# Splitting a 2048-point transform 64 by 32 instead of 128 by 16 in a fused long-convolution and feed-forward kernel

## The chip, the cores and the metric

The kernel runs on one core of a Trainium2 chip. A core has TensorE (PE), which multiplies matrices on an array of 128 rows by 128 columns and writes to eight PSUM banks of 512 float32 columns; VectorE (DVE) and ScalarE (ACT), which work element by element and empty the banks; GpSimd (POOL) and SyncE (SP), which issue most of the transfers. The metric is the device time of one execution in microseconds (us).

## The reference

S = 2048 positions, D = 640 channels, F = 1728 hidden units, all in bfloat16. One layer norm feeds two branches. Branch A multiplies a short causal filter of `k` (four taps for each channel) with `v`, convolves the product along the positions with a filter as long as the sequence (by an FFT of twice the length), adds a skip term and multiplies with the normed input. Branch B is a feed-forward network with gelu, followed by silu. The result is the input plus the product of the branches.

```python
def _A_ref(q, k, v, shift_k, ssm_k, ssm_D):
    k_pad = jnp.pad(k, ((0, 0), (ks - 1, 0), (0, 0)))
    for t in range(ks):
        k_shift = k_shift + k_pad[:, t:t + S, :] * shift_k[:, ks - 1 - t][None, None, :]
    kv = k_shift * v
    kv_f = rfft(pad(kv, S)); kf_f = rfft(pad(ssm_k, S))      # along the positions, length 2 S
    y = irfft(kv_f * kf_f)[:S]                               # in bfloat16
    return q * (y + kv * ssm_D)
def _B_ref(x, w1, b1, w2, b2):
    return gelu(x @ w1 + b1) @ w2 + b2
x = A_q
xn = _layernorm(x)
return x + _A_ref(xn, A_k, A_v, ...) * silu(_B_ref(xn, ...))
```

## The kernel before, in words

**Layout.** Position 16 p + j lies on partition p as row j of 640 channels (`x_v`, `k_v`, `v_v`, `out_v`). `area` is a pool of 48 slots of two such rows; every intermediate of branch A takes a slot (`pair`, `flat`) or a run of columns over two slots (`span`), with a count of uses after which the slot comes free (`Slots`).

**The transform.** The long convolution is a transform in two stages, a product, and the inverse in two stages, all by matmuls.

- *First stage* (`f1`, line 582; steps `kf` for the filter, `uf` for the signal): for each of the 16 rows n2 the 128 partitions are multiplied with a 128x128 matrix of cosines (`WA`) and one of sines (`WB`). A step is one bank, a third of 1280 columns (`EDGES`: 428, 426, 426), and has one or two matmuls. There are 48 steps for each operand. Each step's bank is emptied by `f1_out` on ACT (`.a` in the plan) or DVE (`.d`), and the lines go to DRAM (`scrK`, `scrU`) by POOL's queue.
- *Second stage* (`blocks`, line 445; steps `ff` for the filter, `mu` for the signal, `ma` and `mb` for the inverse): the lines come back from DRAM with 128 of them across the partitions. The transform of 16 points, real and imaginary part, is block-diagonal in blocks of 32, so a step is four matmuls of 32x32 by 512 columns; the digit of `TURNS` says by how many blocks a step rotates its outputs, so that steps next to each other can use different blocks of the array. 40 steps of each of the four kinds make 160 groups, 640 matmuls. `product` on DVE multiplies with the filter (40 times plainly, 40 times with real and imaginary part swapped; `swap_load` makes that copy by DMA).
- *Last stage* (`inv2`, lines 745 and 746; steps `y`): after a third trip through DRAM (`scrC`, `cab_load`), a step sums a matmul with `GA` and one with `GB`, both 128x128. `GA` and `GB` are the memory of `WA` and `WB`, filled anew with the inverse's angles: for each of four parts a product, a mask, a sine, an absolute value and a cosine (`i2_*`). `gate` multiplies the bank with the other branch.

**The short filter.** `kv_step` (lines 611 to 628; steps `cv`) works on two rows at a time: four products with the taps, three sums, one product with `v`, 8 pieces x 8 operations of 1280 elements a partition on DVE. The taps are spread over the partitions by matmuls (`tap`), two in the opening (`prologue`) and two later (`late_tap`, steps `em` and `ee`).

**The feed-forward branch** runs in four chunks of 512 positions: `ffn1` (steps `h`, line 498; the 14th of each chunk, line 494, has 64 hidden units and puts two matmuls of 64 columns side by side), gelu on ACT, `ffn2` (steps `g`, line 531, 14 matmuls of 320 columns), silu on ACT, products on POOL and DVE.

**The order.** Nothing is scheduled at run time. After `prologue`, the text `PLAN` lists some 1,100 steps, and each engine and queue does its share of them in that order. SP's queue does the loads (`X`, `K`, `V`, `C`, `B`, `fl`, `ml`, `mk`, `yl`, `q`), POOL's the stores (`ks`, `us`, `ms`, `ys`). A step that needs a bank or a slot waits until it has been emptied. The plan mixes feed-forward steps with steps of branch A.

Of the kernel before, what the change touches and what calls it, by code (L numbers as in the profile page):

```python
# [34 lines left out]
PLAN = """
ir he0 X1 he1 he2 em6 he3 em7 w h13 em5 K1 ls5 ws1 ls4 ls7 em4 K0 h8 ee6.d ee4.a ls6 h10 ee7.a ee5.a he13 cv16 lv1 lr1
cv1 he4 he8 C2 cv0 h6 cv9 he5 lb1 he6 h7 cv2 h12 ln6.d h11 cv8 ln5.d ln4.a h9 he10 ln7.a tt8 he12 B1 cv17 he11 he9 cv3
he7 cv10 cv18 B0 cv11 cv4 cv19 cv20 tt9 s B2 tt6 tt7 te9.a g3 cv21 te6.d cv22 tt5 C1 ge3 C0 ws2 ss te7.d sm g2 g7 cv12
C3 C4 ge2 kt3 V3 kt5 te5.d kt8 V1 d kc5.d kt10 ws0 kt14 K2 ge7 kc3.a te8.d kc10.d kt0 cv5 kf10 kc8.a kc14.a kf24 kt12
ke24.a kt4 kc12.d kf31 V7 kt6 kf11 kf9 ke10.a K3 kc4.d ke31.a kc0.d ke11.a kf44 kf43 V2 ke44.d kt2 kc2.d kc6.a kf17 X3  # L40
ke9.a kf32 ke32.d kf30 kt11 kf42 kt13 kf37 kt7 kc11.d ke30.a ks10 ke17.a kf38 kc13.d V6 ke42.a ke43.a kt9 ke37.d kf16
kf1 kc7.d kt1 gm3.d kf12 ke38.a ke16.a kc9.d kf36 kt15 kf21 ke1.a ke36.a kc1.d kf6 kf29 gm7.d kc15.d kf39 kf25 ke21.a
X2 cv33 V5 kf20 ke6.a kf41 cv32 V0 cv6 cv24 ks12 ke29.a ks14 cv23 cv13 ke25.a cv34 kf15 ke15.a ke41.a cv56 ke20.a ks5
g5 ke12.a kf7 kf13 ge5 cv57 kf14 kf27 kf8 ke39.a ke27.a kf26 kf40 ke8.a cv41 g0 kf28 ke40.a ks13 ke26.a ke14.a cv40
uf13 kf34 ks3 ke7.a kf19 ge0 cv35 ks8 ue13.a kf18 kf35 ke13.a ke18.a ks4 kf45 g4 ke19.a ks6 gm5.d uf17 cv36 ke45.a kf33
ke34.a ke28.a ks9 ke35.a gm0.d kf0 ke33.a cv7 kf23 cv14 V4 cv58 kf47 cv37 ge4 ke23.a ke0.a kf5 kf22 g6 uf4 ks2 ks11
ke5.a cv42 ke47.a ke22.a ks7 ge6 kf4 kf46 uf5 cv15 ls10 ke4.a cv59 uf15 kf3 ke46.a ks15 kf2 cv38 ke3.a ks1 ke2.a cv25
g1 ue4.a uf0 ks0 ue5.a gm6.d fl0 uf3 ue15.a ue17.a ue3.a uf12 cv43 ue12.a uf14 ue14.a uf16 cv39 ue16.a ue0.a cv26 uf1
ue1.a fl9 h21 us1 uf2 ue2.a ls9 us4 ge1 uf11 gm1.d h15 cv44 cv48 cv45 he21 gm2.d cv46 h25 cv27 uf9 cv60 h19 ue11.a uf27
us5 cv47 h16 he15 cv61 he25 uf28 us0 ue9.a he16 cv28 cv62 uf26 h27 ue28.a uf6 fl3 fl8 h20 ue27.a he19 he20 uf25 h17  # L50
he27 uf29 uf10 h23 h26 ue29.a ue6.a uf8 uf7 ue25.a ue26.a ue10.a cv29 ue8.d cv63 fl4 he17 uf34 ue7.a ue34.a he26 h14
uf33 ff1 fl2 ue33.a he14 cv30 cv49 uf32 uf35 uf46 ue46.a fl1 uf42 he23 h22 ue35.a he22 uf44 uf31 ue31.a h18 cv31 uf23
us9 uf24 ue42.a uf30 cv50 ue44.d cv51 uf43 ue32.a ue43.d ue24.a cv52 he18 uf22 fl13 h24 ls11 ue23.a us2 fl15 cv53 fe1.a
uf21 ff11 ue22.a ff7 ue30.a ff8 ls8 us14 he24 g14 uf47 fe11.a ue21.a uf45 fe7.a uf19 ue45.a cv54 g13 ue47.d ge13 cv55
lv2 ue19.d uf18 uf20 ge14 uf38 uf36 us8 us10 ue20.d us3 uf40 gm4.d us11 ue18.a fl14 fl6 uf39 ue39.d us7 ls13 ue38.a
uf41 uf37 ue37.a g9 ue36.a ff6 fl5 ff12 fl12 us15 ue40.d fl7 lr2 lb2 ff20 ln11.d ff2 ff24 ln9.d us6 us12 ue41.a fe8.a
ge9 gm9.d fe20.d fe12.a ff5 ff0 fe24.a fe2.d g11 fe5.a fe0.a ff14 ls14 ln10.d ff13 ff37 ff38 ff33 ff34 ln8.d fe6.a us13
ge11 mk2 ls12 ml2 fe14.a ff16 g15 tt12 fe34.a tt13 fe16.a gm14.p fe38.a tt14 fe37.d tt11 fe33.a ff10 ff35 te12.d te13.d
ff9 ge15 ff3 ff30 fe13.a ml5 te11.d fe9.a te14.d ml3 ff32 g8 tt10 fe3.a ff19 fe35.d ff17 fe30.a ff4 ml4 fe32.a ff31
fe10.a ls15 ff36 gm15.p mu5 lv3 te10.d fe36.a mk5 fe17.a mp5 fe4.a g12 lr3 ff15 mu13 lb3 fe19.d gm13.p mq5 fe31.a  # L60
ln15.d mp13 mu7 mk3 mk4 ge8 ff39 fl11 mu6 ff18 fe39.a gm8.p fe18.a g10 h40 mu14 ml6 mq6 fl10 mq13 ge12 fe15.a ma5 mp6
mp7 ff22 ge10 mq7 mu10 mp14 ff21 mb5 mu9 mq9 he40 h38 fe21.a mk6 mq14 ml1 me5.a mp9 he38 h37 mq10 fe22.a mp10 h29 q2
mu8 he37 ln13.d mu12 mk1 mq8 ma9 he29 ff27 mq12 ml0 mk0 ff23 mp12 mb9 mu15 h35 mq15 mp8 h32 ml8 h34 mu11 fe27.a me9.a
ln12.a mp15 ma8 he35 he32 ml7 ma7 mb7 ma10 fe23.a he34 mu16 mb8 gm10.p ff25 me7.a me8.a ff26 mp11 h39 mu2 mq16 mk8 mu3
mk13 mb10 gm11.p mp16 h33 mk7 mq11 fe26.a ma11 ml10 ma14 fe25.a ff29 mq2 me10.a mb14 mp2 mp3 mk9 mb11 he39 he33 mu20
me14.a mu1 me11.a mq3 mu4 mq4 fe29.a h41 he41 h28 gm12.p mp4 h31 he28 ma15 mp20 ml13 ma4 ff28 mb15 ml12 mu17 mq20 he31
mb4 mp1 mq1 ma3 mb3 mu0 mp0 me4.a h36 fe28.a mp17 me3.a h30 ml9 mu19 ma13 he36 mq0 ma12 me15.a mq17 ma6 mb12 mb13 ma16
mp19 mb6 mu18 mb16 mu34 ml15 mp18 he30 mk12 me13.a g20 ma17 mq19 mq18 me12.a me16.a mu26 ms4 me6.a ms5 mk10 mq34 mu33
# [868 lines left out]
```

## Time and profile before

| | us |
|---|---|
| median of 2 runs | 191.13 (191.09 to 191.18) |
| the profiled execution | 191.78 |
| its span, first to last instruction | 189.8 |
| busy: PE, DVE, ACT, POOL | 183.3, 171.1, 159.1, 59.5 |

The span is what the profile shows of the program; the profiled execution took 2.0 us more than it, and 0.65 us more than the median. A group's row gives line, engine, operation, output and input tiles, shape and count, then the busy time in us, the mean ns of one, and the idle time just before. The matmuls of PE are pipelined: a matmul's duration in a row is longer than the time from its start to the next one's start, and only the latter adds up.

### The profile page before, as it was taken

The numbers are of one execution on the slowest core, as the hardware profiler recorded it, in microseconds if no ns is written. First come the engines' busy times: TensorE is split into PE (matmuls) and PEld (weight loads), VectorE is DVE, ScalarE is ACT, GpSimd is POOL, SyncE is SP. The second block draws the span as 40 slices with busy tenths as digits, with TensorE's granted clock in tenths as the row PEclk, the third lists the DMA queues.
The fourth block names the chain that finished last, engine by engine and source line by source line (L and its number), as shares of the span: only waits on it lengthen the run. The fifth ranks groups of instructions, "written<-read, shape, count | busy, mean of one in ns | idle before, by whom it ended". The sixth has DMA issues, their size and how long they took to land.

```text
span 189.8 us, 4853 instructions
## 1 busy us (share of the span) xinstructions
PE 183.3 (97%) x1811; PEld 110.0 (58%) x1811; DVE 171.1 (90%) x341; ACT 159.1 (84%) x307; POOL 59.5 (31%) x99
## 2 busy tenths in 40 slices
PE   7999999899999999999999999999999999999992
PEld 2486467787765544466665434467563544677671
DVE  6979999999999999899989999999999950689993
ACT  3469999999999999999988999998789599894031
POOL 8539200013546111266043300046159440001050
PEclk9999999999999999999999999999999999999999
DMA  6999999987998999798599899998988859992165
GB/s 186 397 376 311 363 359 405 380 340 231 391 352 329 254 382 378 234 386 337 178 335 318 266 301 337 310 353 287 343 298 284 287 178 290 402 394 114 38 256 195
DMA packets 26399, 57.67 MB, mean 304 GB/s; under 512 B 3016, under 2 KB 14857, under 8 KB 26376
## 3 DMA queue, kind: packets, MB, share of 16 engines
q1 hardware_dynamic: 21872, 39.65, 61.0%
q0 software_dynamic: 4320, 17.70, 25.1%
q8 instruction: 14, 0.23, 0.5%
q14 instruction: 9, 0.07, 0.1%
q10 hardware_dynamic: 184, 0.01, 0.1%
HBM read 33.76 MB, written 18.35 MB: 275 GB/s over the span
## 4 chain that ended last, share of the span: by engine, by line
PE 75%; DMA 16%; ACT 3%; DVE 2%; issue 1%; SPq 1%; DVEq 0%; ACTq 0%
PE banks L531 28%; PE banks L498 21%; DMA w_sb<-in_B_w_dram 11%; PE banks L582 9%; PE banks L445 8%; DMA area<-in_A_ssm_k_dram 5%; PE banks L746 2%; PE banks L745 2%; PE banks L571 2%; ACT area L143 2%; PE banks L482 1%; ACT hT L510 1%; PE banks L494 1%; DVE xn L555 1%; DVE xn L547 0%
## 5 line engine op out<-in xcount | busy, mean ns | idle before, releaser
L143 ACT CAST area<-banks 128x512 bf16<-128x512 f32 (+3 forms) x162 | 78.8, 618 | 5.5 <-PE banks L445 5.5
L531 PE MATMUL banks<-w_sb,hT 128*128 128x320 bf16 (+1 forms) x462 | 66.0, 295 | 0.1
L531 PEld LDWEIGHTS <-hT 128*128 128x128 bf16 x462 | 43.3, 98 | 19.5 <-issue 3.8
L498 PE MATMUL banks<-xnT,w_sb 128*128 128x512 bf16 x230 | 53.5, 379 | 0.0
L704 DVE TENSOR_TENSOR area<-banks,area 128x512 bf16<-128x512 f32 x80 | 48.6, 682 | 0.8 <-PE banks L445 0.4
L498 PEld LDWEIGHTS <-w_sb 128*128 128x128 bf16 x230 | 21.7, 98 | 25.6 <-issue 2.7
L510 ACT ACTIVATE hT<-banks,b_f 128x512 bf16<-128x512 f32 x52 | 33.9, 706 | 1.8 <-PE banks L498 1.0
L539 ACT ACTIVATE sl<-banks 128x320 bf16<-128x320 f32 (+1 forms) x33 | 14.9, 464 | 12.7 <-PE banks L531 10.9
L626 DVE TENSOR_TENSOR area<-area 128x1280 bf16<-128x1280 bf16 x32 | 25.3, 814 | 0.1
L622 DVE TENSOR_TENSOR area<-area 128x1280 bf16<-128x1280 bf16 x24 | 19.3, 816 | 0.0
L730 POOL DMA_DIRECT2D scrC<-area x16 | 11.8, 737 | 23.2 <-DMA area<-area 18.7
L754 DVE TENSOR_TENSOR area<-banks,xn 128x426 bf16<-128x426 f32 (+1 forms) x18 | 10.0, 595 | 9.1 <-PE banks L746 9.1
L597 POOL DMA_DIRECT2D scrK<-area x16 | 8.8, 555 | 28.7 <-DVE area L144 19.1
L445 PE MATMUL banks<-area,mats 32*32 32x512 bf16 x640 | 17.2, 380 | 0.0
L582 PE MATMUL banks<-area,WA 128*128 128x212 bf16 (+1 forms) x64 | 16.5, 299 | 0.0
L547 POOL TENSOR_TENSOR xn<-xn,sl 128x320 bf16<-128x320 bf16 x14 | 11.2, 808 | 15.6 <-ACT sl L539 10.2
L582 PE MATMUL banks<-area,WB 128*128 128x426 bf16 (+1 forms) x64 | 15.8, 299 | 0.0
L608 POOL DMA_DIRECT2D scrU<-area x16 | 8.6, 543 | 20.9 <-ACT area L143 14.5
L445 PEld LDWEIGHTS <-mats 32*32 32x32 bf16 x640 | 6.4, 88 | 10.1 <-issue 8.2
L763 POOL DMA_DIRECT2D out_dram<-area x6 | 3.3, 551 | 26.5 <-DVE area L759 26.5
L144 DVE CAST area<-banks 128x426 bf16<-128x426 f32 (+3 forms) x18 | 10.9, 611 | 0.7 <-ACT area L143 0.5
L452 DVE BATCH_NORM_STATS2 st<-xn 128x6 f32<-128x320 bf16 x24 | 10.4, 477 | 0.0
(108 smaller groups left out, 209.4 us busy)
## 6 DMA issues: line engine op xcount, KB each, us to landing
scrK<-area POOLq DMA_DIRECT2D x16, 320.0 KB, 4.0
scrU<-area POOLq DMA_DIRECT2D x16, 320.0 KB, 5.1
area<-scrK SPq DMA_DIRECT2D x16, 320.0 KB, 6.6
area<-area SPq DMA_DIRECT2D x32, 160.0 KB, 4.4
area<-scrU SPq DMA_DIRECT2D x16, 320.0 KB, 4.4
scrC<-area POOLq DMA_DIRECT2D x16, 320.0 KB, 4.6
area<-scrC SPq DMA_DIRECT2D x16, 320.0 KB, 6.9
area<-in_A_k_dram SPq DMA_DIRECT2D x4, 640.0 KB, 9.4
```

Source lines behind the costliest of these rows:

```text
L143: return nc.scalar.copy(out=out_ap, in_=in_ap)
L445: nc.tensor.matmul(out=out[b, :], lhsT=mats[a, m, a], rhs=rhs[a, :], start=start, stop=stop)
L498: nc.tensor.matmul(out=ps, lhsT=w1_sb[:, t, ft * P:(ft + 1) * P], rhs=xnT[:, t, :], start=(t == 0), stop=(t == DT - 1))
L510: nc.scalar.activation(out=hT[:, ft, :], in_=one(("h", i)), func=ACT.Gelu_apprx_tanh, bias=b1_f[:, ft:ft + 1], scale=1.0)
L531: nc.tensor.matmul(out=ps[:, 0:ws.stop - ws.start], lhsT=hT[0:M, ft, q * P:(q + 1) * P], rhs=w2_sb[0:M, ft, hs.start + ws.start:hs.start + ...
L539: nc.scalar.activation(out=sl[:, ws], in_=one(key)[:, 0:ws.stop - ws.start], func=ACT.Silu)
L547: mul.tensor_tensor(out=xr[:, ws], in0=xr[:, ws], in1=live["sl", i][:, ws], op=ALU.mult)
L582: nc.tensor.matmul(out=ps[:, dst], lhsT=(WA, WB)[r][:, n2, :], rhs=rows[:, n2 % 2, src], start=True, stop=True)
L622: nc.vector.tensor_tensor(out=uc, in0=uc, in1=tmp, op=ALU.add)
L626: nc.vector.tensor_tensor(out=tmp if s else uc, in0=kh[:, r0:r0 + KC, :], in1=w_exp[:, j:j + 1, :].to_broadcast([P, KC, D]), op=ALU.mult)
L704: nc.vector.tensor_tensor(out=p_part(i, x), in0=full(one(("mu", i)), i), in1=span(name, i), op=ALU.mult)
L730: nc.gpsimd.dma_start(out=pair_view(scrC)[g2], in_=pair(("c", g2)))
```

## The change

The 2048 points are split as 64 by 32 instead of 128 by 16. Position 32 p + 16 h + j lies on partition 64 h + p, so each half of the partitions holds the 64 positions of one parity h of the block of 16.

- *First stage*: a matmul multiplies the 64 rows of one half with a 64x128 matrix `W`, whose columns alternate cosine and sine of 64 frequencies. Step i of 48 has half h = i mod 2; the number of matmuls and their columns stay. The angle tables are half as wide.
- *Second stage*: the transform of 32 points with its two parts has blocks of 64 (`QB = 64`), so a group is two matmuls of 64x64 by 512 columns. `TURNS` has other digits, of which the parity counts.
- *Last stage*: a matmul has all 128 rows and 64 columns (`G`), one for each half of the output partitions; nothing is summed over two matmuls. `G` is memory of its own, and the absolute value and the cosine of its angles are gone.
- *Transposes of the long filter* (`k_tr`): ten of 64 columns in place of five of 128.
- *Short filter*: four rows at a time, 4 x 8 operations of 2560 elements, on pairs of slots (`quad`).
- *Taps*: all four in the opening; the matmuls that warm the array go from 13 to 10. `late_tap` is gone.
- The loads and stores have the halves as a dimension of their own; `line_view` takes the new order of lines.
- `PLAN` is another order of the steps.

```diff
-WARM = (6, 7)
+WARM = (6, 2, 2)
-TURNS = "302320120133202130013212102100231320131321131323"
+TURNS = "301231320003111003222231123023122231130022030123"
...
+w X1 h11 B1 ws0 ls7 he5 K0 he11 ls6 ls5 ls4 B0 lv1 lr1 he0 he2 h9 lb1 ln6.d ln5.d he1 ln7.d cv1 h13 he4 cv0 h6 C0 cv2
+ln4.a h10 he13 he6 h8 s he9 tt9 B2 cv3 C3 he8 h12 he10 he12 h7 tt6 he3 tt7 tt8 C1 C2 he7 te9.a cv4 ss g6 ws1 cv5 g5 ge6
+te7.a tt5 te5.d C4 g0 ge5 ws2 kt7 te6.d kc7.d X3 kt6 kt9 te8.a ge0 kt8 kt5 K2 kt4 kc6.a K1 V7 kc9.a kc5.d kc4.d K3
+kc8.a kt11 gm5.d kt2 V3 kf19 kf23 kc2.d kf28 ke28.a kt13 kf13 d ke23.a kf18 kc11.d ke19.a kt1 kf21 ke18.a kf20 sm kc1.d
...
-    x_v = A_q[0].rearrange("(p j) d -> p j d", j=NJ)
+    x_v = A_q[0].rearrange("(p h j) d -> h p j d", h=2, j=NJ)
...
-    def line_view(scr):
-        return scr.rearrange("(r n c) d -> r n c d", c=2, n=NJ)
+    def line_view(scr, i):
+        m, h = divmod(i, 2)
+        return scr.rearrange("(r h m t) d -> r h m t d", h=2, m=NJ // 2, t=2)[:, h, m, :, :]
...
-    WA = consts.tile([P, NJ, P], BF16, name="WA")
-    WB = consts.tile([P, NJ, P], BF16, name="WB")
-    GA, GB = WA, WB
+    W = consts.tile([P, NJ, P], BF16, name="W")
+    G = consts.tile([P, NJ, P], BF16, name="G")
-    QB = 32
+    QB = 64
+    HP = P // 2
-    SPANNED = ("kin", "K", "ks", "uin", "c")
+    SPANNED = ("kin", "K", "ks", "uin", "c", "v", "uc", "tm")
...
         for t in range(DT):
-            nc.tensor.transpose(out=tp[:, t * P:(t + 1) * P], in_=kf_v[:, t, i, :], identity=ident[:])
+            for h in range(2):
+                nc.tensor.transpose(out=tp[h * HP:(h + 1) * HP, t * P:(t + 1) * P], in_=kf_v[:, t, i, h, :], identity=ident[:])
...
+    def f1_at(i):
+        m, r = divmod(i, 6)
+        j, h = divmod(r, 2)
+        return m, h, j
     def f1(name, i, rows):
-        n2, j = divmod(i, 3)
+        m, h, j = f1_at(i)
         ps = one((name, i))
+        hp = slice(h * HP, (h + 1) * HP)
         for r, src, dst in parts(j):
-            nc.tensor.matmul(out=ps[:, dst], lhsT=(WA, WB)[r][:, n2, :], rhs=rows[:, n2 % 2, src], start=True, stop=True)
+            nc.tensor.matmul(out=ps[:, dst], lhsT=W[hp, 2 * m + r, :], rhs=rows[hp, r, src], start=True, stop=True)
...
+    def quad(name, i, uses=1):
+        a0, a1 = (slots.take((name, 2 * i + x), uses) for x in range(2))
+        v = area[:, 2 * a0:2 * a0 + 2, :]
+        return bass.AP(v.tensor, v.offset, [list(v.ap[0]), [2 * D * (a1 - a0), 2], [D, 2], [1, D]])
     def kv_step(i):
...
-            r0 = 3 + i * KC - j
-            nc.vector.tensor_tensor(out=tmp if s else uc, in0=kh[:, r0:r0 + KC, :],
-                                    in1=w_exp[:, j:j + 1, :].to_broadcast([P, KC, D]), op=ALU.mult)
+            r0 = 3 + i * KR - j
+            nc.vector.tensor_tensor(out=tmp if s else uc, in0=kh[:, r0:r0 + KR, :].rearrange("p (a b) d -> p a b d", a=2),
+                                    in1=w_exp[:, j:j + 1, None, :].to_broadcast([P, 2, 2, D]), op=ALU.mult)
...
-    def i2_abs(i):
...
-    def i2_cosine(i):
...
     def inv2(i):
...
-            nc.tensor.matmul(out=ps[:, dst], lhsT=GA[:, n2, :], rhs=cab[:, 0, src], start=True, stop=False)
-            nc.tensor.matmul(out=ps[:, dst], lhsT=GB[:, n2, :], rhs=cab[:, 1, src], start=False, stop=True)
+            for h in range(2):
+                hp = slice(h * HP, (h + 1) * HP)
+                nc.tensor.matmul(out=ps[hp, dst], lhsT=G[:, 2 * m + r, hp], rhs=pair(("cab", 2 * m + h))[:, r, src],
+                                 start=True, stop=True)
...
+        taps(0, 2)
+        warm(WARM[2])
...
+        tap_out(0)
+        tap_out(1)
         norm_dve(0)
...
+        taps(2, 4)
```

More of the change, by code (lines that the diff above doesn't have):

```diff
@@ L44 @@
[L44 to L48, printed above, removed]
@@ L413, in small_phase @@
+        nc.gpsimd.tensor_scalar(out=koff[:], in0=c_in, scalar1=float(L // 4), scalar2=float(3 * L // 4), op0=ALU.mult,
+                                op1=ALU.add)
     def small_phase():
@@ L565, in last_store @@
         hs = slice(0, D) if q < CH - 1 else hs
[L566 removed]
+        nc.sync.dma_start(out=out_v[:, :, c * CH + q, hs], in_=xn_tiles[c][:, q, hs])
     def k_tr(i):
@@ L596, in k_store @@
     def k_store(n2):
-        nc.gpsimd.dma_start(out=line_view(scrK)[:, n2, :, :], in_=pair(("ko", n2)))
+        nc.gpsimd.dma_start(out=line_view(scrK, n2), in_=pair(("ko", n2)))
         slots.drop(("ko", n2))
@@ L676, in tap @@
                          start=True, stop=True)
-    def late_tap(i):
-        tap(i // 2, i % 2, one(("em", i)))
-    def late_tap_out(i, eng):
-        evac(eng, w_exp[:, i // 2, half(i % 2)], one(("em", i))[:, 0:HALF])
-        ones.drop(("em", i))
     def uin_load(g2):
@@ L762, in out_store @@
     def out_store(i):
-        nc.gpsimd.dma_start(out=out_v[:, 2 * i:2 * i + 2, :], in_=pair(("o", i)))
+        nc.gpsimd.dma_start(out=out_v[:, :, 2 * i:2 * i + 2, :], in_=pair(("o", i)))
         slots.drop(("o", i))
@@ L779, in sq @@
         def sq(a):
-            nc.scalar.activation(out=sd[:, a:a + 2], in_=mv[:, a:a + 2, 1], func=ACT.Sqrt, bias=eps[:])
+            nc.scalar.activation(out=sd[:, a:a + 2], in_=mv[:, a:a + 2, 1], func=ACT.Sqrt, bias=LN_EPS)
         def rc(a):
@@ L789, in tap_out, with taps @@
         def tap_out(j):
-            nc.scalar.copy(out=halves(w_exp[:, j, :]), in_=banks[:, 2 * j + 2:2 * j + 4, 0:HALF])
+            b = 2 + 2 * (j % 2)
+            nc.scalar.copy(out=halves(w_exp[:, j, :]), in_=banks[:, b:b + 2, 0:HALF])
+        def taps(lo, hi):
+            for j in range(lo, hi):
+                for h in range(2):
+                    tap(j, h, banks[:, 2 + 2 * (j % 2) + h, :])
         def warm(n, bank=7):
@@ L851, in prologue @@
         turn(1)
-        for j in range(2):
-            for h in range(2):
-                tap(j, h, banks[:, 2 * j + 2 + h, :])
+        taps(2, 4)
         bn(2, 0)
```

235 lines of the change are left out of this document (114 added, 121 removed).

## The prediction

> **What bounds the kernel now.** I read the page first, then who waits on TensorE, then the stages, then the costliest groups.
>
> ```profile
> PE 183.3 (97%) x1811; PEld 110.0 (58%) x1811; DVE 171.1 (90%) x341; ACT 159.1 (84%) x307; POOL 59.5 (31%) x99
> PEclk9999999999999999999999999999999999999999
> PE 75%; DMA 16%; ACT 3%; DVE 2%; issue 1%; SPq 1%; DVEq 0%; ACTq 0%
> ```
>
> TensorE (PE) is busy nearly all the time at full clock, and three quarters of the chain that ended last are its work. Busy matmuls overlap, so this alone doesn't say that PE is the bound. The list of PE's waits and four stages do:
>
> ```profile
> PE banks L794 <- POOL ident masks.py:199: 1.4, 1, 1.4
> PE banks L571 <- DVE area L672: 0.7, 1, 0.7
> PE banks L812 <- DMA w_sb<-in_B_w_dram: 0.3, 1, 0.3
> 30.00:40.00 10.00, 9.22 (x100) 7.65 (x98) 9.96 (x23) 9.95 (x17) 0.00 (x0) 1.00 1.02 390
> 60.00:70.00 10.00, 10.00 (x59) 5.04 (x58) 9.97 (x18) 9.93 (x21) 2.08 (x4) 1.00 0.95 312
> 120.00:130.00 10.00, 9.98 (x133) 6.03 (x129) 10.00 (x18) 9.97 (x20) 3.46 (x5) 1.00 0.98 340
> 150.00:160.00 10.00, 10.00 (x59) 4.96 (x57) 4.41 (x6) 9.87 (x18) 3.19 (x4) 1.00 0.69 223
> ```
>
> PE waited three times: twice in the opening, once, for 0.7 us, at the first transpose of the long filter. The columns of a stage are its length, then PE, PEld, DVE, ACT, POOL busy. VectorE and ScalarE are full too between 30 and 130 us, but PE never waits for them: the written order always has a feed-forward matmul at hand. So the time is the length of PE's stream:
>
> ```profile
> 16.63 0.44 PE L675 MATMUL banks<-skT,ident 4*128 4x320 bf16 x2
> 182.01 4.01 PE L531 MATMUL banks<-w_sb,hT 128*128 128x320 bf16 x42
> ```
>
> The written order's first matmul starts at 16.63, the last ends at 186.02; 169.4 us lie between, 16.6 before and 3.8 (silu, product, store) behind, together the span of 189.8. I forecast what the change does to the 169.4.
>
> **The price of one matmul, and of a change of form.**
>
> ```profile
> L531 PE MATMUL banks<-w_sb,hT 128*128 128x320 bf16 x403 | 59.9, 299 | 0.1
> L582 PE MATMUL banks<-area,WA 128*128 128x212 bf16 (+1 forms) x64 | 16.5, 299 | 0.0
> L582 PE MATMUL banks<-area,WB 128*128 128x426 bf16 (+1 forms) x64 | 15.8, 299 | 0.0
> L745 PE MATMUL banks<-area,WA 128*128 128x428 bf16 (+3 forms) x32 | 8.6, 299 | 0.0
> L746 PE MATMUL banks<-area,WB 128*128 128x428 bf16 (+3 forms) x32 | 8.5, 298 | 0.0
> L445 PE MATMUL banks<-area,mats 32*32 32x512 bf16 x640 | 17.2, 380 | 0.0
> 43.53 1.90 PE banks L531 x14
> 151.55 4.32 PE banks L498 x20
> 104.52 3.41 PE L498 MATMUL banks<-xnT,w_sb 128*128 128x512 bf16 x15
> 107.87 0.72 PE L445 MATMUL banks<-area,mats 32*32 32x512 bf16 x28
> 108.52 3.41 PE L498 MATMUL banks<-xnT,w_sb 128*128 128x512 bf16 x15
> 116.38 0.74 PE L494 MATMUL banks<-xnT,w_sb 128*64 128x256 bf16 x10
> 117.05 1.25 PE L498 MATMUL banks<-xnT,w_sb 128*128 128x512 bf16 x5
> ```
>
> In the stream a 320-column matmul costs 1.90/14 = 136 ns, a 512-column one 4.32/20 = 216 ns. First stage (L582) and last stage (L745, L746) have the same mean duration as the 320-column ones, and 320 columns on average, so 128 x 136 = 17.4 us and 64 x 136 = 8.7 us.
>
> Blocks of the array work side by side. Ten 64-column matmuls of 256 columns (L494) take 117.05 - 116.38 = 0.67 us: as five pairs at half of 216 they are 0.54, and 0.13 is left. Twenty-eight 32x32 matmuls of 512 columns take 0.65, where one after another they would take 6.0: sixteen fit at once, so they are two passes, 0.43. What is left over is the change of form. Before it the fifteen L498 take 107.87 - 104.52 = 3.35 against 15 x 0.216 = 3.24. I price each change at 0.1 us (0.11 going in, 0.13 to 0.22 coming out together with a pass's staggered starts).
>
> **The change, part by part.**
>
> *First stage.* As many matmuls with as many columns, but on 64 rows: two in different halves can run together. The halves alternate with the step number (even lower, odd upper), and the order on PE was not laid out in pairs: kf19, kf23, kf28, kt13, kf13, kf18. I walked the written order, 26 unbroken stretches, with the rule that a matmul starts no sooner than the one written before it, nor before its half is free. It gives 11.8 us; perfect pairing would be 8.7, none 17.4. No row has two row halves over the same columns; I take 11.8, since the 32x32 blocks do run in different rows at once: -5.6.
>
> *Last stage.* Again 64 matmuls, each on 64 columns, and its two halves written next to each other, as in L494: 8.7 becomes 4.35, -4.3. A step now needs both line loads of its pair, which the order puts ahead of it: nothing.
>
> *Second stage.* 160 groups of four 32x32 become 160 groups of two 64x64. Four old groups filled the array in a pass, only two new ones do. Full passes would be 160/4 x 0.216 = 8.6 before and 160/2 x 0.216 = 17.3 after. The seven groups at 107.87 are two passes; seven of the new ones are four or more. Counted through the orders, stretch by stretch with the turns (only their parity counts now), it is about 56 passes before, 12.0 us, and 94 after, 20.2: +8.2. The count before, with 22 stretches x 0.22 for their ends, is 16.8 and the row shows 17.2 busy. This is the part that eats the two gains.
>
> *Changes of form.* Before: 22 second-stage stretches, four of 64 columns (h13, h27, h41, h55) and the late taps make 52 changes. After: first stage, transposes of the filter and last stage have forms of their own, and I count 106. 54 more at 0.1 are +5.4. The rows show changes to and from the full array only; between two partial forms I take the same, and nothing as the lower bound.
>
> [...]
>
> *Taps.* Four late ones leave the stream (-0.5).
>
> ```profile
> 8.26 0.58 ACT L143 COPY xnT<-banks 128x512 bf16<-128x512 bf16 x1 [1.85 <-PE banks L803]
> 8.74 1.30 ACT L790 CAST area<-banks 128x640 bf16<-128x640 f32 x2
> ```
>
> In the opening they take the place of warming matmuls, and their two evacuations, 1.3 us, fit into ScalarE's idle 1.85 ahead of the copy at 8.26; if not, they delay the first block by at most that 1.3. I take nothing.
>
> *Transposes of the filter.* 80 become 160 half as wide, in pairs: the same 80 places if pairs run together.
>
> *VectorE.*
>
> ```profile
> L626 DVE TENSOR_TENSOR area<-area 128x1280 bf16<-128x1280 bf16 x32 | 25.3, 814 | 0.1
> L622 DVE TENSOR_TENSOR area<-area 128x1280 bf16<-128x1280 bf16 x24 | 19.3, 816 | 0.0
> L615 DVE TENSOR_TENSOR area<-area 128x1280 bf16<-128x1280 bf16 x8 | 6.5, 818 | 0.0
> L547 DVE TENSOR_TENSOR xn<-xn,sl 128x320 bf16<-128x320 bf16 x17 | 5.2, 316 | 0.2 <-ACT sl L539 0.2
> L338 DVE TENSOR_TENSOR area<-area 128x2048 int32<-128x2048 f32 x1 | 2.3, 2294 | 0.7 <-POOL area L337 0.7
> L342 DVE TENSOR_SCALAR area<-area 128x2048 int32<-128x2048 int32 x1 | 1.2, 1229 | 0.0
> L361 ACT ACTIVATE area<-area,half_l 128x2048 f32<-128x2048 int32 x1 | 2.0, 2014 | 0.0
> L663 ACT ACTIVATE area<-area,half_l 128x512 f32<-128x512 int32 x4 | 2.9, 722 | 0.1
> ```
>
> From 320 to 1280 elements 0.50 us: 0.52 ns an element and 0.15 fixed. 64 operations become 32 of 2560 elements at 1.48, 47.4 instead of 52.2: -4.8; half-wide angle products another -1.7. On ScalarE eight operations of the last stage's angles go (8 x 0.72 = 5.8) and three sines halve (about -2.6). All of it is credited at nothing: PE's waits list shows that no PE instruction of the middle is late for either engine. If four-row access patterns ran at half the rate, VectorE would gain 32 x 1.33 = 43 us of work; I give that no case, since their inner rows stay 640 contiguous elements.
>
> *Loads and queues.* Transfers keep their sizes and number; the last filter load is now ahead of K1 and K2 on SP's queue, one 640 KB load fewer before it. So PE's 0.7 us wait at L571 should go (-0.7); VectorE's second filter block waits longer for K1, behind which stands only its own list. POOL does as many small operations for the angles, and the row step moved from the first place to the middle is off PE's path.
>
> Sum: -5.6 - 4.3 + 8.2 + 5.4 - 0.5 - 0.7 = +2.5 us. The profiled execution took 191.78 (span 189.8 and 2.0 around it); 194.3 against it. The median shown, 191.13, is 0.65 under the profiled one, so 193.6.
>
> **The rivals.**
>
> *VectorE and ScalarE bound the middle after all.* For it: both stand at 9.9 to 10 in the stages from 30 to 130, and the planned order hides feed-forward matmuls among them, so a lighter VectorE may let the whole order close up. 4.8 + 1.7 = 6.5 off, with PE absorbing the rest: 191.1 - 6.5 = 184.6. Against: PE's stream has no hole to close. It decides only if my counts of passes and changes are too high by 6 us or more. 15%.
>
> *The row halves run one after the other.* Both use all 128 columns, and no row shows that. Then the first stage stays at 17.4: +5.6, 199.2. From about a quarter of that loss on the kernel is over 2% slower (2.5 + 1.4 = 3.9). 15%.
>
> *Half-width transposes don't pair.*
>
> ```profile
> 39.29 0.48 PE L571 MATMUL banks<-ident,area 128*128 128x128 bf16 x5
> L571 PE MATMUL banks<-ident,area 128*128 128x128 bf16 x80 | 7.0, 227 | 0.8 <-DVE area L672 0.7
> L494 PEld LDWEIGHTS <-w_sb 128*64 128x64 bf16 x40 | 1.9, 109 | 1.2 <-issue 1.2
> L531 PEld LDWEIGHTS <-hT 128*128 128x128 bf16 x429 | 40.1, 98 | 18.3 <-issue 3.8 <-ACT hT L510 0.2
> ```
>
> Five transposes now take (0.48 - 0.227)/4 = 63 ns each. A 64-column load takes 109 ns, no less than 98 for twice the columns; if 160 transposes go singly at 63 ns, that is 80 x 63 = +5.0, 198.6. Against: L494's loads hide behind its pairs. 10%. [...]
>
> **How the numbers follow.** The forecast's own case has 60%: 190 to 196.5, where the low end lets changes between partial forms cost less, and the high one the second stage's turns collide more or a new wait of 3 us appear. The change doing nothing of weight falls inside it. Two per cent, about what a measurement of this kernel tells from no change, is 187.3 and 195.0. Of the 60, 10 lie above 195.0. Faster: 15. Slower: 15 + 10 + 10 = 35. Within: 50. The range leaves out the first rival and the upper half of the second: 188.2 (no new change of form is paid: 193.6 - 5.4) to 199.
>
> **What would show it.** The second stage's busy time rises from 17.2 to about 25, 320 matmuls; the last stage's falls from 17.1 to about 9; first-stage matmuls in pairs start a few ns apart. VectorE falls to about 165, ScalarE to about 151, and PE stays at 97% or more with no wait in the middle. I am wrong if PE shows holes, if VectorE's sum doesn't fall, or if first-stage matmuls of different halves start 136 ns apart.

## The result and the profile after

The changed kernel takes 391.78 us (median of 2 runs, 391.0 to 392.57) against 191.13: 2.05 times as long, interval 2.03 to 2.07. The forecast was 193.6, the range 188.2 to 199.0. (Executions of two kernels below, the one with natural rows and its variant with blocks of 32, come in two kinds about 3 us apart, 201.06 against 204.2 to 204.3 and 200.5 to 201.4 against 204.0 to 204.2; of these the shorter kind is compared.) The page of the profile after, its busy times, four of the rows in 40 slices and the chain that ended last by engine:

```profile
span 389.2 us, 4313 instructions
PE 207.8 (53%) x1568; PEld 114.0 (29%) x1568; DVE 171.4 (44%) x309; ACT 157.7 (41%) x301; POOL 60.7 (16%) x100
PE   5269218992000001800079999997099994089500
PEclk9559686997555555865569999999589998579955
DMA  1832464127111111421139677944667544680530
GB/s 42 228 123 90 132 207 164 54 110 288 53 52 52 51 50 50 157 96 50 49 124 340 249 301 275 328 156 129 183 221 256 193 177 126 175 312 17 143 89 31
...
DMA 29%; SPq 29%; PE 25%; DVE 6%; ACT 3%; issue 2%; DVEq 0%; ACTq 0%
```

PE was busy 97% of the span and is now busy 53%; it stands still for whole slices, and the chain is 58% transfers and SP's queue where it was 75% PE. In those slices the DMA row reads 1, and the rate is 50 to 53 GB/s, slice after slice. The stretches of 20 us show it with the share of the 16 DMA engines (columns: length, then PE, PEld, DVE, ACT, POOL busy, PE's granted clock, DMA share, GB/s):

```profile
100.00:120.00 20.00, 0.00 (x0) 0.00 (x0) 2.89 (x2) 0.00 (x0) 0.00 (x0) 0.50 0.13 52
120.00:140.00 20.00, 0.00 (x0) 0.00 (x0) 0.00 (x0) 0.00 (x0) 0.00 (x0) 0.50 0.13 51
```

A share of 0.13 is what two engines of sixteen give (2/16 = 0.125), which the profile doesn't name one by one. For 40 us such transfers carry everything, PE, ACT and POOL stand still, and VectorE works 2.9 us. PE waits for VectorE, and VectorE for loads of `v` and `k`; first PE's waits after, then VectorE's (total us, times, longest):

```profile
PE banks L588 <- DVE area L630: 96.8, 2, 64.3
```

```profile
DVE area L630 <- DMA area<-in_A_v_dram: 69.2, 2, 36.0
DVE area L641 <- DMA area<-in_A_k_dram: 29.8, 1, 29.8
```

The transfers themselves: the loads of `v` after, and then before (duration on the issuing queue in ns, least, median and most):

```profile
L279 SPq DMA_DIRECT2D area<-in_A_v_dram x8: 6344/6731/17257, 77.1 to 172.1; - x8
```

```profile
L283 SPq DMA_DIRECT2D area<-in_A_v_dram x8: 327/365/905, 26.0 to 46.4; - x8
...
DMA to landing us min/median/max: 4.9/6.2/7.7
```

They have the same 320 KB and number as before, but the issue of each now takes SP's queue 6.3 to 17.3 us, where it took 0.3 to 0.9. Everything behind it in the queue comes later too. What differs is the shape: `x_v`, `k_v`, `v_v` and `out_v` now have the halves as outermost dimension, of size 2.

### The profile page after: what moved, and what is told of

Its sections match the earlier page's. It is cut to its first block, busy times and chain, and to the rows that moved or that the text cites. A ratio compares the mean times of both kernels' runs of the same rounds, so it can differ in the third digit from the quotient of the medians.

```text
span 389.2 us, 4313 instructions
## 1 busy us (share of the span) xinstructions
PE 207.8 (53%) x1568; PEld 114.0 (29%) x1568; DVE 171.4 (44%) x309; ACT 157.7 (41%) x301; POOL 60.7 (16%) x100
## 4 chain that ended last, share of the span: by engine, by line
DMA 29%; SPq 29%; PE 25%; DVE 6%; ACT 3%; issue 2%; DVEq 0%; ACTq 0%
DMA area<-in_A_k_dram 13%; SPq L279 12%; PE banks L497 9%; PE banks L530 8%; DMA area<-in_A_v_dram 6%; PE banks L444 5%; DMA w_sb<-in_B_w_dram 4%; DMA area<-scrC 4%; DMA area<-scrU 3%; SPq L269 3%; SPq L303 3%; SPq L296 3%; ACT area L141 2%; SPq L299 2%; SPq L274 2%
## 5 line engine op out<-in xcount | busy, mean ns | idle before, releaser
L141 ACT CAST area<-banks 128x426 bf16<-128x426 f32 (+2 forms) x154 | 75.4, 595 | 116.8 <-PE banks L588 99.9
L530 PE MATMUL banks<-w_sb,hT 128*128 128x320 bf16 (+1 forms) x462 | 70.6, 309 | 9.7 <-DMA w_sb<-in_B_w_dram 9.6
L588 PE MATMUL banks<-area,W 64*128 64x212 bf16 (+3 forms) x128 | 19.2, 316 | 97.2 <-DVE area L630 96.8
L497 PE MATMUL banks<-xnT,w_sb 128*128 128x512 bf16 x230 | 55.6, 391 | 0.2
L530 PEld LDWEIGHTS <-hT 128*128 128x128 bf16 x462 | 44.5, 102 | 35.5 <-DMA w_sb<-in_B_w_dram 9.7
L641 DVE TENSOR_TENSOR area<-area 128x2560 bf16<-128x2560 bf16 x16 | 23.5, 1487 | 42.2 <-DMA area<-in_A_k_dram 29.8
L588 PEld LDWEIGHTS <-W 64*128 64x128 bf16 x128 | 7.1, 96 | 107.5 <-DVE area L630 97.5
L630 DVE TENSOR_TENSOR area<-area 128x2560 bf16<-128x2560 bf16 x4 | 6.0, 1490 | 69.3 <-DMA area<-in_A_v_dram 69.2
L444 PE MATMUL banks<-area,mats 64*64 64x512 bf16 x320 | 27.7, 400 | 11.9 <-DMA area<-scrU 9.6
L444 PEld LDWEIGHTS <-mats 64*64 64x64 bf16 x320 | 10.2, 108 | 27.0 <-issue 12.8
L637 DVE TENSOR_TENSOR area<-area 128x2560 bf16<-128x2560 bf16 x12 | 17.9, 1490 | 0.2
L745 PE MATMUL banks<-area,G 128*64 128x212 bf16 (+3 forms) x64 | 6.8, 345 | 16.1 <-DMA area<-scrC 16.1
L142 DVE CAST area<-banks 128x512 bf16<-128x512 f32 (+2 forms) x22 | 13.9, 644 | 3.4 <-PE banks L588 1.7
```

The lines of the kernel that those rows point to most:

```text
L141: return nc.scalar.copy(out=out_ap, in_=in_ap)
L142: return nc.vector.tensor_copy(out=out_ap, in_=in_ap)
L444: nc.tensor.matmul(out=out[b, :], lhsT=mats[a, m, a], rhs=rhs[a, :], start=start, stop=stop)
L497: nc.tensor.matmul(out=ps, lhsT=w1_sb[:, t, ft * P:(ft + 1) * P], rhs=xnT[:, t, :], start=(t == 0), stop=(t == DT - 1))
L530: nc.tensor.matmul(out=ps[:, 0:ws.stop - ws.start], lhsT=hT[0:M, ft, q * P:(q + 1) * P], rhs=w2_sb[0:M, ft, hs.start + ws.start:hs.start + ...
L588: nc.tensor.matmul(out=ps[:, dst], lhsT=W[hp, 2 * m + r, :], rhs=rows[hp, r, src], start=True, stop=True)
```

## The experiments

**Theory and rivals at the start.** The theory, from the share of 0.13 at 52 GB/s: a transfer with an outermost dimension of two is carried by two DMA engines, and that alone makes the 200 us. The rival: the new order or the new stages wait for something of their own, and the slow loads follow from it. A second question is what the change costs once its transfers are mended.

### The transfers' shape

The changed kernel, each such load and store as two transfers of 64 partitions (shown for `k`; the others alike):

```diff
-nc.sync.dma_start(out=kh[:, 3 + r0:3 + r0 + KR, :], in_=k_v[:, :, r0:r0 + KR, :])
+for g in range(2):
+    nc.sync.dma_start(out=kh[g * HP:(g + 1) * HP, 3 + r0:3 + r0 + KR, :], in_=k_v[g, :, r0:r0 + KR, :])
```

> The changed kernel with each load and store of the permuted rows issued as two transfers of 64 partitions instead of one whose first dimension is the two halves; all matmuls, operations and the order stay. Theory A (a transfer whose outermost dimension is two is carried by two of the sixteen DMA engines, which is the 52 GB/s and the share of 0.13 between 100 and 140 us): the loads of k land in about 10 us, the waits for in_A_k and in_A_v are gone, and the time falls to what the TensorE stream gives, 193.6 us by the sum of the prediction (188 to 199). Rival B (the half-array matmuls or the new order stall the kernel, and the transfers are late because of it): no change, 380 to 395 us. Rival C (the permuted rows themselves are slow to read, whatever the shape of the transfer): 350 us or more.

Measured 210.97 us, ratio to before 1.102 (1.097 to 1.108). Of the 200.7 us lost (391.8 - 191.1), 180.8 go with this edit; rivals B and C fall. But 211 lies above the 188 to 199 of theory A, so the shape is not the whole of it. Then with `k` and `v` alone:

> The changed kernel with only the loads of k and v issued as two transfers of 64 partitions; the loads of the input rows and the stores keep the halves as first dimension. Theory A: 5.2 MB of k and v at 52 GB/s are about 101 us of the 200 lost; the input rows (2.6 MB at first, 2.6 MB again for the last sum, 2.6 MB stored) stay at two engines: 270 to 320 us, and the stages with 52 GB/s are now those of the input rows. Rivals B and C: 380 to 395 us.

That is the same edit at the loads of `k` and `v` only. One run, 313.39, inside the 270 to 320 of theory A: 78.4 us go with `k` and `v`, the other 102.4 with the loads of `x` and the stores of the output. The counterpart is the kernel before, with nothing of the change but the views (shown for `x`; `k`, `v`, the output and the loads follow):

```diff
-x_v = A_q[0].rearrange("(p j) d -> p j d", j=NJ)
+x_v = A_q[0].rearrange("(p h j) d -> h p j d", h=2, j=NJ)
```

> The kernel before with nothing changed but the views of x, k, v and out, which take the halves as first dimension (position 32p+16h+j on partition 64h+p); the rows then stand on other partitions than its transform means, so it convolves a permuted sequence, with the same amount of work. Theory A: the same loads at two engines, 330 to 420 us, with k and v loads landing after 40 us or more and no change on TensorE. Rival B: 191 us. Rival C: about as A; the first run tells A from C.

One run, 379.43. Its rows in 40 slices have the same stretches of 50 to 53 GB/s at a DMA digit of 1:

```profile
DMA  2812154813411115111169878949826124961441
GB/s 62 217 51 91 52 169 122 295 52 141 176 52 52 52 69 217 51 53 50 50 231 362 302 288 288 293 157 302 311 107 250 69 82 144 306 241 54 91 126 36
```

So the shape does it without any new stage or order: the rival of the start falls. That a dimension of 2 gives two engines is inferred from the traces: share 0.13, 52 GB/s, or 26 for each of two; all sixteen, further down, move 420 at a share of 1.03, or 26 each. Outermost dimensions of 64 and 128 fill all sixteen (share 1.03 for both in the kernel of loads further down); what other sizes do was not run.

### Why two transfers still cost 10 us and more

The kernel before, each of those transfers as two of 64 partitions and nothing else:

```diff
-nc.sync.dma_start(out=kh[:, 3 + r0:3 + r0 + KR, :], in_=k_v[:, r0:r0 + KR, :])
+for g in (slice(0, 64), slice(64, P)):
+    nc.sync.dma_start(out=kh[g, 3 + r0:3 + r0 + KR, :], in_=k_v[g, r0:r0 + KR, :])
```

> The kernel before, unchanged but that each load and store of x, k, v and out is issued as two transfers of 64 partitions (natural rows, result unchanged). It asks whether the repair used in the run with two transfers has a price of its own. Theory A2 (a transfer to 64 partitions, though carried by all sixteen engines, moves fewer bytes a second than one to 128): the rate between 10 and 40 us falls from 341 to 390 GB/s to below 310 at full share, the last filter load lands 3 us or more later than at 32.9 us, 194 to 203 us. Rival: only the issues cost (25 more on SyncE's queue of about 0.4 us), which has room: 190.5 to 193 us.

204.23 us, ratio 1.065 (1.059 to 1.070): halves cost the old kernel 13 us, at the upper end of what theory A2 said (194 to 203); its rival (190.5 to 193) falls. The stretch from 20 to 30 us, in the kernel before, in this one, and in the changed one with two transfers:

```profile
20.00:30.00 10.00, 10.00 (x72) 6.02 (x71) 9.88 (x16) 9.95 (x17) 1.05 (x1) 1.00 1.05 367
```

```profile
20.00:30.00 10.00, 7.12 (x44) 3.46 (x43) 6.26 (x13) 5.85 (x10) 1.04 (x1) 1.00 1.04 309
```

```profile
20.00:30.00 10.00, 9.11 (x64) 4.83 (x63) 5.65 (x9) 9.95 (x17) 1.05 (x1) 1.00 1.05 274
```

All 16 DMA engines are full each time (share 1.04 to 1.05), and move 367, 309 and 274 GB/s: the same engines do less in the same time. Two ideas for that were tried in the kernels: the halves on two queues, so that both are under way together (changed kernel with two transfers, lower half on SP's queue, upper half on POOL's), and every second partition in place of neighbouring ones (kernel before).

```diff
-    nc.sync.dma_start(out=kh[g * HP:(g + 1) * HP, 3 + r0:3 + r0 + KR, :], in_=k_v[g, :, r0:r0 + KR, :])
+    (nc.sync, nc.gpsimd)[g].dma_start(out=kh[g * HP:(g + 1) * HP, 3 + r0:3 + r0 + KR, :], in_=k_v[g, :, r0:r0 + KR, :])
```

> The changed kernel with two transfers of 64 partitions for each load of x, k and v, the lower half from SyncE's queue and the upper from GpSimd's, so that both halves are under way at once. Theory A2: the rate between 10 and 40 us rises from 269 to 290 to 320 GB/s or more, TensorE's waits for w2 (1.9) and for the filter (2.2 us) shrink, 203 to 208 us instead of 211. Rival (the order of the loads, with their bytes, makes the waits): 209 to 213 us.

219.85 us, 1.149 (1.144 to 1.154), against the expectation: slower than on one queue. From 10 to 40 us it moves 259 to 274 GB/s at a share of 1.04 to 1.07; two queues don't bring the rate back here. The time itself tells less: POOL's queue has work of its own ahead of the loads, so the first upper half of `k` goes out at 19.8 us and the lower one at 9.7.

```diff
-for g in (slice(0, 64), slice(64, P)):
+for g in (slice(0, P, 2), slice(1, P, 2)):
```

> The kernel before with each load and store of x, k, v and out as two transfers of 64 partitions again, but of every second partition instead of a half each (natural rows, result unchanged). Issues, sizes and rows are as in the run of the kernel before with halves, 204.2 us. [...] Rival A3 (twice as many transfers of half the size cost it, wherever they lie): 202 to 206 us.

The idea was that the place of the 64 partitions counts: 340 GB/s or more between 10 and 40 us and a time of 190.5 to 194 us. Measured 234.71 us, 1.224 (1.218 to 1.230): the idea and its rival both missed. Its loads of `v`, and its stretches from 30 to 50 us:

```profile
L286 SPq DMA_DIRECT2D area<-in_A_v_dram x16: 471/596/607, 44.5 to 88.4; - x16
...
DMA to landing us min/median/max: 2.6/2.7/6.1
```

```profile
30.00:40.00 10.00, 7.04 (x42) 3.89 (x41) 9.93 (x18) 6.57 (x10) 0.00 (x0) 0.83 1.04 358
40.00:50.00 10.00, 5.73 (x48) 4.34 (x46) 3.70 (x9) 3.15 (x4) 0.00 (x0) 0.84 0.25 87
```

The transfers land fast (2.7 us in the median). The engines are full from 30 to 40 us, at 358 GB/s, but it is the filter's whole transfers that SP's queue issues there (from 30.9 us on). The loads of `v` are issued from 44.5 to 88.4 us where the kernel before issued them from 26.0 to 46.4. SP's queue waits ahead of them (its waits, total us, times, longest):

```profile
SPq L286 <- PE banks L586: 16.2, 3, 7.4
...
SPq L286 <- DVE mats L428: 9.5, 1, 9.5
```

At its `v` loads the kernel before has 1.6 us of the first (one time, L582 there) and none of the second. The lateness begins earlier: the first load of `k` goes out at 17.25 us, with halves at 6.00. And PE's transposes of the long filter wait for loads of `v`, which they don't read:

```profile
PE banks L575 <- DMA area<-in_A_v_dram: 18.2, 5, 5.3
```

So loads and other work on `area` wait for each other; why the strided slices bring that is not settled. The edit changed two things, the partitions and the time of issue, and its time tells nothing of the rate. The rate was then measured by itself: a kernel that only loads `k` and `v` in pieces of 640 KB into four buffers one after the other, and stores 16 rows.

```diff
+    forms = [
+        (whole, (slice(0, P),), SP),
+        (halved, (slice(0, 64), slice(64, P)), SP),
+        (second, (slice(0, P, 2), slice(1, P, 2)), SP),
+        (queues, (slice(0, 64), slice(64, P)), (nc.sync, nc.scalar)),
+    ]
...
+            for r in range(0, 2 * NJ, R):
+                src = (k_v, v_v)[r // NJ][:, r % NJ:r % NJ + R, :]
+                for g, eng in zip(groups, engines):
+                    eng.dma_start(out=tile_[g, r:r + R, :], in_=src[g])
```

> This kernel computes nothing: it loads k and v four times into four buffers, one buffer after the other (a one-element copy of each row stands between them), in 8 pieces of 640 KB each, and then stores 16 rows as output. First buffer: 128 partitions in one transfer. Second: each piece as two transfers of 64 neighbouring partitions on one queue. Third: as two transfers of every second partition. Fourth: 64 neighbouring partitions each, on two queues. Nothing else uses the DMA engines, and no buffer is waited for but by that copy. Theory (which partitions a transfer writes sets its rate; neighbouring 64 reach it only in part): first and third buffer 340 to 400 GB/s in the middle of their loads, second 240 to 320, fourth like the second, all at a DMA share near 1. Then the 234.7 us with every second partition came from the later issues alone (v's first load at 44.5 us instead of 30.0). Rival (a transfer of half as many partitions is slower whichever they are, by its size or its number of packets per engine): third like the second, both 240 to 320. Second rival (the rate is lost only where other transfers run beside them): all four within 5%.

Stretches of 2 us from each of the four (columns: length, DVE and POOL busy, clock, DMA share, GB/s), in the order given, two from the third:

```profile
12.00:14.00 2.00, 0.00 (x0) 0.00 (x0) 1.00 1.03 420
...
26.00:28.00 2.00, 0.00 (x0) 0.00 (x0) 1.00 1.03 228
...
46.00:48.00 2.00, 0.00 (x0) 0.00 (x0) 1.00 0.97 310
...
54.00:56.00 2.00, 0.00 (x0) 0.00 (x0) 1.00 1.01 417
...
72.00:74.00 2.00, 0.00 (x0) 0.00 (x0) 1.00 1.03 297
```

128 partitions 420 GB/s; 64 neighbouring ones 228; every second one 282 to 325 between 44 and 50 us and then 392 to 420 to the end; two queues with one half each 233 to 236 between 64 and 68 us and 284 to 300 later. The 16 engines are full in all of them but for a few stretches of the third (share 0.87 to 0.97). Why the third begins slower is not shown. The copies between the buffers waited 16.4, 25.2 and 17.4 us for the first three (the first counts from the start of the program):

```profile
L67 DVE COPY second<-halved 128x32 bf16<-128x32 bf16 x1 | 0.2, 248 | 25.2 <-DMA halved<-in_A_v_dram 25.2
L67 DVE COPY queues<-second 128x32 bf16<-128x32 bf16 x1 | 0.3, 251 | 17.4 <-DMA second<-in_A_v_dram 17.4
L67 DVE COPY halved<-whole 128x32 bf16<-128x32 bf16 x1 | 0.2, 248 | 16.4 <-DMA whole<-in_A_v_dram 16.4
```

The theory holds in kind: the first form lies above its 340 to 400 GB/s, the second at or under the low end of its 240 to 320, and the third reaches its 340 to 400 only in its second part, but needs 17.4 us for what takes the second 25.2. So it is neither the size nor the number of transfers (the third form has both of the second), nor other traffic, but which partitions a transfer writes. 228 of 420 is 0.54, and transfers of every second partition reach 392 to 420 in the second part of their load. The rows that are read are hardly the cause: in the changed kernel with two transfers each half reads every second block of 16 rows, in the kernel before with halves neighbouring ones, and from 10 to 20 us, where other loads run too, these move 269 and 257 GB/s (shares 1.09 and 1.06), the kernel before 341 (1.03). By what way the partitions set the rate is not shown.

### What the change is worth with whole transfers

The changed kernel on the row order of before, so that its transfers cover 128 partitions again (shown for `x`; the other views and the loads follow):

```diff
-x_v = A_q[0].rearrange("(p h j) d -> h p j d", h=2, j=NJ)
+x_v = A_q[0].rearrange("(p j) d -> p j d", j=NJ)
```

> The changed kernel with the views of x, k, v and out of the kernel before: single transfers of 128 partitions, sixteen engines. The rows then stand on other partitions than its transform means, so it convolves a permuted sequence; matmuls, operations and order are those of the change. This is the change without its transfers. By the prediction's sum 193.6 us; with the transposes at 112 ns a pair (3.9 us more) 197.5. Theory (the sum, mended by the transposes): 195 to 200 us. Rival 1 (VectorE's and ScalarE's lighter load closes the order up once the loads are in time): below 189 us. Rival 2 (the order has waits of its own): above 202 us.

Then the same with the five full-width transposes of before (shown for the first of the two kernels that have them; the other is the changed kernel with two transfers):

```diff
-for h in range(2):
-    nc.tensor.transpose(out=tp[h * HP:(h + 1) * HP, t * P:(t + 1) * P], in_=kf_v[:, t, i, h, :], identity=ident[:])
+nc.tensor.transpose(out=tp[:, t * P:(t + 1) * P], in_=kf_sb.rearrange("p t (a b) -> p t b a", b=NJ)[:, t, i, :], identity=ident[:])
```

> The run with natural rows, and the long filter transposed by 80 matmuls of 128 columns as in the kernel before (the filter's positions are permuted as the signal's are). Theory: 16 x 5 x (0.112 - 0.063) = 3.9 us and up to 14 changes of form (1.4 us) less on TensorE's stream, 3 to 5.5 us under the run with natural rows. Rival (ScalarE and VectorE, which empty the transposes' banks, bound that stage): no difference within 1 us.

> The run with two transfers, and the transposes of the long filter undone: 80 of 128 columns in place of 160 of 64. The rows of the transposed filter then stand in natural order and not by halves, so the filter that is convolved is a permuted one; the work is the same. The rival of the prediction on the transposes holds in a milder form: pairs of 64 columns start together, but a pair takes 112 ns where one of 128 columns took 63. So 16 x 5 x (0.112 - 0.063) = 3.9 us and some changes of form should go: 205 to 207.5 us. Rival (that stage waits for the loads anyway): 210 to 211.5 us.

With the natural rows: 201.06 us, above the 195 to 200 of the theory; of the rivals, below 189 falls, and the waits that the other means are not in the trace, where PE waits once behind the opening, for 0.7 us. With full transposes as well: 197.09, ratio 1.032 (1.026 to 1.037). With two transfers the full transposes bring nothing, 212.38 beside 210.97, against the theory: in the profiled executions PE's waits for the filter's loads grow from 1.9 to 4.2 us, and the first matmul behind the opening starts 3.5 us later (21.70 for 18.19). TensorE's order in the kernel with natural rows, then in that with full transposes as well:

```profile
34.46 4.68 PE L571 MATMUL banks<-ident,area 128*64 128x128 bf16 x80
39.07 0.53 PE L588 MATMUL banks<-area,W 64*128 64x428 bf16 x3
```

```profile
31.22 2.65 PE L570 MATMUL banks<-ident,area 128*128 128x128 bf16 x40
33.80 0.53 PE L587 MATMUL banks<-area,W 64*128 64x428 bf16 x3
```

Eighty half-width transposes take 39.07 - 34.46 = 4.61 us, 58 ns each; forty full ones 2.58, 65 ns each. By their start times the halves do go in pairs, 0 to 7 ns apart; but the next pair starts some 109 ns later, where full ones follow each other after 62. So a pair costs nearly two full ones. Weight loads of halves are longer too (203 ns on average in the changed kernel, 148 for full ones in the kernel before); whether they set the pace is not shown. On 160 for 80 it is 160 x 0.058 - 80 x 0.065 = 4.1 us, and 201.06 - 197.09 is 4.0.

The spans of these two profiles differ by 7.2 us (202.5 and 195.3). Of that, 3.2 lie ahead of the rows shown (34.46 for 31.22), in the opening; its first blocks with natural rows alone, and with full transposes:

```profile
10.17 4.41 PE L819 MATMUL banks<-xnT,w_sb 128*128 128x256 bf16 x25
```

```profile
8.52 2.90 PE L818 MATMUL banks<-xnT,w_sb 128*128 128x256 bf16 x25
```

The same 25 matmuls take 4.41 us in one and 2.90 in the other, and start 1.65 us later. Both kernels have the same opening, with 10 warming matmuls and the taps among them, where before has 13. The granted clock reads 1.00 from 0 to 20 us in both, so the profile shows no lower clock there; the cause is open.

### The second stage's blocks

The changed kernel with two transfers, blocks of 32 as before (`QB = 32`) and the digits of before in `TURNS`:

> The run with two transfers, and the second stage back in four 32x32 blocks with the turns of the kernel before (half of each block's inputs are left out, the bytes, columns and evacuations are the same). By the count of passes, 94 against 56, 8.2 us leave TensorE's stream: 202 to 204.5 us if the stream is the bound there, 209 to 211.5 us if VectorE's products are.

The digits of `TURNS` belong to the old order of steps; in the new order they give 91 passes of my count, so this was no test: 212.34 us beside 210.97. It was repeated with natural rows and digits looked for in the new order (66 passes):

```diff
-QB = 64
+QB = 32
-TURNS = "301231320003111003222231123023122231130022030123"
+TURNS = "000321203203113112023132102133100321012121131323"
```

> The run with natural rows, and the second stage in four blocks of 32 with turns looked for in this order (half of each block's inputs are left out; bytes, columns, evacuations and order are the same). The run with the turns of the kernel before wasn't a test: those turns give 91 passes in this order, 19.7 us, as many as the 64x64 blocks. These give 66 passes, 14.2 us against 20.2. Theory (TensorE's stream is the bound there): 5 to 7 us under the run with natural rows. Rival (VectorE's products bound the second stage): no difference within 1.5 us.

200.47 to 201.35 us: no gain beside 201.06. The theory (5 to 7 us) misses, and the time is as the rival has it. The groups with blocks of 64 (natural rows) and of 32:

```profile
L444 PE MATMUL banks<-area,mats 64*64 64x512 bf16 x320 | 25.5, 384 | 0.8 <-DVE area L142 0.7
```

```profile
L444 PE MATMUL banks<-area,mats 32*32 32x512 bf16 x640 | 23.3, 381 | 1.9 <-DVE area L704 0.7 <-DVE area L142 0.7 <-ACT area L141 0.3
```

2.2 us less busy and 1.1 us more idle. From start to start the stage takes 25.0 us with blocks of 64 and 24.3 with blocks of 32, in 23 stretches each: 0.7 less, where 28 passes fewer had been priced at 6.0. So the count of passes doesn't price this stage in the new order. That VectorE's products hold it, as the rival says, is not shown either: PE's waits for them are 0.7 us. What does hold it stays open.

### The taps alone

The kernel before with the taps in the opening, in sets of two:

```diff
-WARM = (6, 7)
+WARM = (6, 5, 0)
+        taps(0, 2)
...
+        taps(2, 4)
```

> The kernel before with one part of the change alone: all four taps made in the opening (two sets of four matmuls in place of warming matmuls, their outputs copied out there), and the late taps' steps out of the order. Theory (TensorE's stream sets the time, and what leaves it is gained): the late taps' matmuls leave the order and 0.5 to 0.9 us go, 190.3 to 190.8 us beside 191.2 of the kernel before, where the opening's clock stays up. Rival (the opening has no room): its two further copies and four matmuls delay the first blocks by as much, 191.2 or more; with the opening at half clock 194.

191.06 us beside 191.33 (12 and 17 runs), ratio 0.9998 (0.9978 to 1.0018). In its profiled execution the last stretch of PE begins at 181.02 us, where before it began at 182.01:

```profile
181.02 4.01 PE L531 MATMUL banks<-w_sb,hT 128*128 128x320 bf16 x42
```

That execution was its fastest (190.53), and PE's stream in it is 0.6 us shorter (168.8 from 16.26 us on, for 169.4), as the theory has it; but the medians are 0.3 us apart and the interval reaches from -0.4 to +0.3 us, so theory and rival are not told apart by the time: no change that can be measured.

## Why the prediction was wrong

**The step that failed** is the one under "Loads and queues": "Transfers keep their sizes and number". That is so, and the shape was never asked about. The diff puts the halves outermost in all four views, and every load of `x`, `k` and `v` and every store of the output goes from 16 DMA engines to two, by the share of 0.13. Taken at nothing, it costs 180.8 us beside two transfers of 64 partitions, and 190.7 beside whole ones (391.8 - 201.1). An estimate from the rates measured: the five passes over arrays of 2.62 MB (`x` twice, `k`, `v`, the output) are 13.1 MB; at 52 GB/s they take 252 us, at 420 they take 31. The difference, 221, is what the DMA engines lose; the kernels lost 181 (changed) and 188 (before with the views, 379.4 - 191.2), which is less; that part of the 221 lies beside other work is argued, not shown. No rival named transfers at all.

**Mended, it would still have been wrong**, by less: the changed kernel with two transfers takes 211.0, above the range. The way there, each step a run:

| | us | step |
|---|---|---|
| before | 191.3 | |
| new stages and order, whole transfers, full transposes | 197.1 | +5.8 |
| half-width transposes | 201.1 | +4.0 |
| transfers of 64 partitions | 211.0 | +9.9 |
| transfers by two engines | 391.8 | +180.8 |

The prediction had +2.5 for the first two together.

**The terms of PE's stream.** These are sums of the times from each matmul's start to the next one's, from the first one after the opening, in us; a change of form falls to the line ahead of it. "Mended" is the kernel with natural rows and full transposes.

| | before | mended | measured | predicted |
|---|---|---|---|---|
| first stage | 18.6 | 17.5 | -1.1 | -5.6 |
| second stage | 16.1 | 25.0 | +8.9 | +8.2 |
| last stage | 8.7 | 5.0 | -3.7 | -4.3 |
| feed-forward | 115.4 | 117.4 | +2.0 | 0 |
| transposes of the normed input | 3.6 | 3.7 | +0.1 | 0 |
| late taps | 0.7 | 0 | -0.7 | -0.5 |
| transposes of the filter | 6.3 | 6.0 | -0.3 | 0 (and -0.7 for the wait) |
| 54 changes of form | | | in the lines | +5.4 |
| stream | 169.4 | 174.6 | +5.2 | +2.5 |

The first matmul after the opening comes 0.7 us sooner (15.88 for 16.63) and the end behind the last one is 1.1 longer (4.9 for 3.8); with the stream that makes the 5.5 between the spans (195.3 and 189.8), within the rounding.

- *Second and last stage* came near their prices, and so did their busy times: 25.5 us for 320 matmuls (about 25 was said), and for the last stage the four rows below (mended kernel). The second stage's agreement is partly luck: its price was a count of passes, and taking the passes back with blocks of 32 gave back 0.7 us, not 6.0. So larger blocks are not shown to be what its 8.9 us are.

```profile
L744 PE MATMUL banks<-area,G 128*64 128x426 bf16 x16 | 2.6, 346 | 0.0
L744 PE MATMUL banks<-area,G 128*64 128x428 bf16 x16 | 2.5, 346 | 0.0
L744 PE MATMUL banks<-area,G 128*64 128x212 bf16 x16 | 2.0, 263 | 0.0
L744 PE MATMUL banks<-area,G 128*64 128x214 bf16 x16 | 1.9, 255 | 0.0
```

 That is 9.0 us together (about 9 was said).
- *First stage.* The two row halves do run together, so that rival falls: in the changed kernel with two transfers

```profile
60.31 0.72 PE L592 MATMUL banks<-area,W 64*128 64x428 bf16 x8
60.96 2.08 PE L533 MATMUL banks<-w_sb,hT 128*128 128x320 bf16 x14
```

 eight of them take 60.96 - 60.31 = 0.65 us, where eight at 136 ns are 1.09; in the mended kernel such pairs start 2 to 7 ns apart. But over all steps only 1.1 us of the 5.6 is left. The prediction's walk, done again over the 26 stretches of the mended kernel, gives the same 11.8 us, and the starts give 17.5. A lone matmul of 426 columns at 37.01 us takes 0.29 to the next start where its columns are worth 0.18; at 0.1 for each stretch's end that is an estimate of 2.6 of these 5.7. One stretch, from 39.61 us on, takes 2.9 where the walk says 1.3. The rest is not parted. All lines together lie 8.1 us above their own terms, where 5.4 was booked for changes of form; that is the 2.7 by which the sum of +2.5 falls short of +5.2. That all 54 changes are paid, those between two partial forms too, was the author's estimate: no run shows the price of one of these, only the 8.1 us over all lines.
- *Transposes.* "The same 80 places if pairs run together": the pairs do start together, and need 109 ns where a full one needs 62. The third rival, at 10%, had +5.0 for halves that go singly; it is 4.0, and not by the way that the rival says, so its size came near by luck.
- *VectorE and ScalarE at nothing*: no gain came of either, and the first rival falls. The short filter costs 23.5 + 17.9 + 6.0 = 47.4 us in the mended kernel, as worked out, but VectorE as a whole is at 170.1 (165 said, 171.1 before), because other groups grew: emptying banks with a change of type by 2.9 us (22 for 18) and the normalising of the input by 1.8 among them. ScalarE is at 155.8 (151 said). PE's waits in the mended kernel show only one of 0.7 us behind the opening:

```profile
PE banks L444 <- DVE area L142: 0.7, 1, 0.7
```

- *Taps*: their 0.7 us leave the stream, where 0.5 was said; the time of the run with the taps alone doesn't show it.
- *The signs to look for* were the right ones: "wrong if PE shows holes", and PE shows holes of 64 us; "if VectorE's sum doesn't fall", and it is 171.4 in the changed kernel for 171.1. What they lacked was a line on the DMA share.
